# Eight rows of five gradient stores issued from ScalarE in place of GpSimd

## The chip, the core and the metric

The kernel runs on one core of a Trainium2 chip. Its five engines work beside each other, each through its own instructions in order: TensorE (PE) multiplies matrices, VectorE (DVE) and ScalarE (ACT) do element-wise work, GpSimd (POOL) and SyncE (SP) here do little but issue DMAs. A DMA is issued by an engine, is carried by sixteen DMA engines that all issuers share, and reports on a semaphore when it has landed. SBUF is the on-chip memory with 128 partitions (rows), PSUM holds what TensorE produces. The metric is the device time of one execution in microseconds (us), as the median over runs.

## The reference

Attention of one query per head over 8192 keys, and its gradients. There are B x H = 2 x 32 = 64 heads; K and V of a head are 8192 x 128 bf16, which is 2 MB each.

```
scores = einsum("bhqd,bhkd->bhqk", q, k) * d**-0.5
p      = softmax(scores)
out    = einsum("bhqk,bhkd->bhqd", p, v)
dq, dk, dv = vjp(out)(grad_out)
```

With one query row, dv of a head is the outer product of p with grad_out, and dk is the outer product of dS with q, where dS is p times (dP minus its weighted mean) times the scale. So K and V are each read once (268 MB in all), and dK and dV, of the same size, are written once.

## The kernel before

**Tiling.** A head's K is one tile `kvt` of 128 partitions x 64 rows x 128 (16 KB on each partition), and V likewise. Twelve such tiles (`NTILE`) live in SBUF, so six heads are resident. Work is cut into slots. Each head has eight of them (`SL`): in slot r, TensorE transposes one quarter of K (r = 0 to 3) or of V (r = 4 to 7) with eight transposes (L239), ScalarE copies the result from PSUM to SBUF (`ev`, L241), and one slot later TensorE multiplies that copy with the query or with grad_out (`score_chunk`, L260). There are two PSUM buffers for the transposes and two SBUF buffers for the copies. In between run softmax pieces, the sums that give out and dq (`acc`, L420; `pick`, `join`), and the outer products (`outer`, L475 on VectorE), which overwrite a quarter of the V tile or of the K tile in place with dv or dk.

**The pipeline.** The loop at L506 goes through all slots, and in each slot deals with up to four heads at different stages. Head i's dv quarters are formed in its slots 9 to 12 (`O1`), its dk quarters in its slots 13 to 16 (`O0`), counted from its first slot. Each tile is stored when its last quarter is done, and the slot of SBUF that it leaves is loaded again with a tile of head i + 6 (`AHEAD`). A K tile and a V tile take turns in one buffer (`slot_of`): V of head i + 6 goes where K of head i was. A load therefore waits until the store of the tile there has landed.

**Who issues what.** `pin` keeps each engine's instructions in the order of the program. SP issues all loads (L114, one 2 MB DMA each), and for the last head the stores in quarters and the two small results dq and out (L585). GpSimd issues the stores of all other heads (L493). So SP's queue of loads waits on stores, and GpSimd's queue of stores waits on VectorE. ScalarE issues no DMA; per slot it makes one copy of 1.0 us and now and then a small one (`window`, L215) or the exponential (L322).

**The five special dk stores.** For heads 6, 17, 28, 39 and 50 (`SPREAD`) the dk store is cut by partitions. `by_rows` issues rows 8 to 127 with `max_dma_last_dim` set (1920 KB), then rows 0 to 2, 3 to 5 and 6 to 7 as three DMAs of 48, 48 and 32 KB without it (L104). [...] 

**The semaphores of DMAs.** As the records in the trace name them, the DMAs that SP issues carry eight semaphores in turn, and those of GpSimd eight others in turn. A DMA waits for the one that carried its semaphore before, eight DMAs earlier.

Of the kernel before, what the change touches and what calls it, by code (L numbers as in the profile page):

```python
# [21 lines left out]
FIRST = 5  # L22
SPREAD = {
    i: ((8, 128, True), (0, 3, False), (3, 6, False), (6, 8, False)) for i in range(6, 56, 11)
}
BACK = {i + 1: FIRST for i in SPREAD}

@with_exitstack
def kernel(  # L30
# [11 lines left out]
    nc = tc.nc  # L42
    B, H, Sq, D = q.shape
# [5 lines left out]
    NT = Sk // P  # L49
# [6 lines left out]
    store_eng = nc.gpsimd  # L56
    pin = tc.keep_in_program_order
# [30 lines left out]
    def turn(n):  # L88

        if n:  # L90
            parts = turns.pop()
            pin(store_eng.dma_start(out=parts[:n, :], in_=q_rows[:n, : 2 * QT], max_dma_last_dim=2 * QT))
        else:
            pin(store_eng.inc_swdge_sem([], [], mode="reset_dge_cursor"))

    def by_rows(dst, src, steps):

        for step in steps:
            if len(step) == 1:
                turn(*step)  # L100
                continue
            p0, p1, cut = step
            cap = {"max_dma_last_dim": NT * D} if cut else {}
            pin(store_eng.dma_start(out=dst[p0:p1], in_=src[p0:p1], **cap))  # L104

    def load(i, w, pieces=(NCH,)):
        h = heads[i]
        t = kvp.tile([P, NT, D], BF16, tag=f"kv{slot_of(i, w)}", name="kvt")
        h.tile[w] = t
        src = (v_v if w else k_v)[i]  # L110
        c = 0
        for m in pieces:
            n0, n1 = c * CH, (c + m) * CH
            pin(load_eng.dma_start(out=t[:, n0:n1, :], in_=src[:, n0:n1, :]))  # L114
            c += m
# [1 line left out]
    load(0, 0, (1, 1, 2))  # L117

    q_rows = q.rearrange("b h s d -> (b h s) d")
    NTURN = len(BACK) + sum(len(step) == 1 and step[0] > 0 for x in SPREAD.values() for step in x)  # L120
    parts_all = const.tile([CH, NTURN, 2 * QT], BF16, name="parts_all")
    turns = [parts_all[:, n, :] for n in range(NTURN)]

    qd_nat = evp.tile([P, CH, P], BF16, tag="ev", name="qd_nat")
    for w, a in enumerate((q, grad_out)):
        rows = a.rearrange("b h s d -> (b h s) d")
        r0 = FIRST if w == 0 else 0
        if r0:
# [3 lines left out]
                    out=qd_nat[:r0, w, :], in_=rows[:r0], max_dma_last_dim=D  # L132
# [28 lines left out]
    for g in range(SG):  # L161
        nc.vector.tensor_copy(
            out=sel4[g * SW : (g + 1) * SW, :, g // 2, :],
            in_=ident_f[g * SW : (g + 1) * SW, g * SW : g * SW + 2 * NCH].rearrange(
                "p (c t) -> p c t", t=2
            ),
# [9 lines left out]
    for w in range(2):  # L176
        nc.vector.tensor_copy(
            out=qd_pair[:BH, w],
            in_=qd_nat[:BH, w, :]
# [22 lines left out]
    def begin(i):  # L202

        h = heads[i]
        sw = ps_sdp.tile([P, 2 * NT + 2 * P + 4], F32, tag="s", name="sw")
        h.score = (sw[:, 0:NT], sw[:, NT : 2 * NT])
        h.s, h.dp = h.score
        h.mT = sw[0:1, 2 * NT : 2 * NT + P]
        h.qbp = sw[:, 2 * NT + P : 2 * NT + 2 * P]
        h.lsum = sw[:, 2 * NT + 2 * P : 2 * NT + 2 * P + 2]  # L210
        h.mb = sw[:, 2 * NT + 2 * P + 2 : 2 * NT + 2 * P + 3]

    def window(i, w):

        pin(nc.scalar.copy(out=qwin[:, w, :, Q0 : Q0 + 2], in_=qpair[:, w, i]))  # L215

    def broadcast(i, w):

        h = heads[i]
        pin(  # L220
            nc.tensor.matmul(  # L221
                h.qbp,
                lhsT=qT[:, w, i : i + 1].to_broadcast([P, P]),
                rhs=ident_bf,
                start=True,
                stop=True,
            )
        )
        h.qb[w] = small.tile([P, D], BF16, tag=f"qb{w}", name="qb")
        pin(nc.vector.tensor_copy(out=h.qb[w][:], in_=h.qbp))  # L230

    def transpose_chunk(i, c):
        w, c = divmod(c, NCH)
        src = heads[i].tile[w]
        tp = ps_tp.tile([P, CH // 2, P], F32, tag="tp", name="tp")
        for m in range(CH // 2):
            n0 = c * CH + 2 * m
            two = src[:, n0 : n0 + 2, :].rearrange("p n d -> p (n d)").bitcast(F32)
            pin(nc.tensor.transpose(tp[:, m, :], two, ident_f[:]))  # L239
        ev = evp.tile([P, CH // 2, P], F32, tag="ev", name="ev")  # L240
        pin(nc.scalar.copy(out=ev[:], in_=tp[:]))  # L241
        return ev
# [26 lines left out]
    def keep_raw(i):  # L269

        h = heads[i]
        h.rows = work.tile([P, QT * P], F32, tag="rows", name="rows")
        pin(nc.vector.tensor_copy(out=h.rows[:], in_=h.raw[:]))  # L273
# [195 lines left out]
    def outer(i, w, c, ends):  # L469

        h = heads[i]
        n0 = c * CH
        shape = [P, CH, D // 2, 2]
        pin(
            nc.vector.tensor_tensor(  # L475
                out=h.tile[w][:, n0 : n0 + CH, :].rearrange("p n (e t) -> p n e t", t=2),
                in0=h.qb[w][:]
                .rearrange("p (e t) -> p e t", t=2)
                .unsqueeze(1)
                .to_broadcast(shape),  # L480
                in1=h.pair[w][:, n0 : n0 + CH, :].unsqueeze(2).to_broadcast(shape),
                op=ALU.mult,
            )
        )
        if c + 1 in ends:
            at = ends.index(c + 1)
            b0, b1 = (ends[at - 1] if at else 0) * CH, (c + 1) * CH
            dst = (dv_v if w else dk_v)[i]
            if w == 0 and i in SPREAD:
                by_rows(dst, h.tile[w], SPREAD[i])  # L490
            else:
                eng = load_eng if len(ends) > 1 else store_eng
                pin(eng.dma_start(out=dst[:, b0:b1, :], in_=h.tile[w][:, b0:b1, :]))  # L493
# [12 lines left out]
    for g in range(SL * BH + O0 + NCH + 4 - SL):  # L506
        now = [(g // SL - b, g % SL + b * SL) for b in range(4)]
        now = [(i, r) for i, r in now if 0 <= i < BH]

        def at(r0):  # L510

            return next((i for i, r in now if r == r0), None)

        def within(r0):

            return next(((i, r - r0) for i, r in now if r0 <= r < r0 + NCH), None)

        if (i := at(O1 + NCH)) is not None and i + AHEAD < BH:
            load(i + AHEAD, 0)
        if (i := at(O0 + NCH)) is not None and i + AHEAD < BH:  # L520
            load(i + AHEAD, 1)
        if x := within(O1):
            outer(x[0], 1, x[1], last if x[0] == BH - 1 else whole)
        if (i := at(O1 + NCH)) in BACK:
            turn(0)
            turn(BACK[i])
        if x := within(O0):
            outer(x[0], 0, x[1], last if x[0] == BH - 1 else whole)
        ev = None
        if g < SL * BH:  # L530
            i, r = divmod(g, SL)
            if r == NCH:
                begin(i)
                broadcast(i, 1)
            if r == NCH + 2:
                broadcast(i, 0)
            ev = transpose_chunk(i, r)
        if (i := at(A1 + NCH + 2)) is not None:
            join(i, 1)
        if (i := at(A0 + NCH + 2)) is not None:  # L540
            join(i, 0)
        if x := within(A1):
            acc(x[0], 1, x[1])
        if x := within(A0):
            acc(x[0], 0, x[1])
        if (i := at(NCH + 1)) is not None:
            spread_rows(i, 0)
        if (i := at(SL + 1)) is not None:
            spread_rows(i, 1)
        if (i := at(NCH + 3)) is not None:  # L550
            max_spread(i)
            expo(i)
        if prev is not None:
            score_chunk(*prev)
        prev = (g // SL, g % SL, ev) if ev is not None else None
        if (i := at(NCH + 1)) is not None and i + 1 < BH:
            window(i + 1, 0)
        if (i := at(1)) is not None and i > 0:
            window(i, 1)

        if (i := at(NCH)) is not None:
            keep_raw(i)
        if (i := at(SL)) is not None:
            keep_raw(i)
        if (i := at(NCH + 1)) is not None:
            max_part(i)
        if (i := at(NCH + 2)) is not None:
            max_all(i)
        if (i := at(NCH + 4)) is not None:
            normalise_p(i)  # L570
        if (i := at(SL + 1)) is not None:
            weigh(i)
        if (i := at(SL + 2)) is not None:
            normalise_ds(i)
        if (i := at(A1 + NCH)) is not None:
            pick(i, 1)
        if (i := at(A0 + NCH)) is not None:
            pick(i, 0)
# [37 lines left out]
```

## Time and profile before

| | |
|---|---|
| median of 3 runs | 1267.52 us (1266.84 to 1269.59) |
| the profiled execution | 1267.85 us |
| its span, first to last instruction | 1266.1 us |
| TensorE busy | 1187.7 us, 94% |
| VectorE busy | 1031.3 us, 81% |
| ScalarE busy | 557.2 us, 44% |
| GpSimd busy | 80.6 us, 6% |
| moved by DMA | 538.53 MB, mean 425 GB/s |

The profiled execution's own time is 1.75 us over its span, and 0.33 us over the median. The transfers are almost evenly split: SP's queue carries 272.70 MB, GpSimd's 264.25 MB. Store DMAs of 2 MB land 44.9 us (median) after they are issued, loads 20.1 us after. A busy TensorE is not TensorE at its peak, since its matmuls are pipelined and their ends are modelled. Times in views of the trace are microseconds from the span's start. In a timeline, the columns are the start, the time taken, the engine, the line, and the operation with what it writes and reads; in brackets stands how long its engine sat idle before it, and what ended that. "SPq" is SP's queue of instructions.

### The profile page before, as it was taken

The page shows a single profiled execution, that of the slowest core. Times are in us where ns is not written, and L with a number is a line of the kernel's source. Part 1 is how long each engine was busy: PE and PEld are TensorE (multiplying, and loading weights), DVE is VectorE, ACT ScalarE, POOL GpSimd, SP SyncE. Part 2 cuts the span into 40 slices and gives each one's busy share as a digit, 9 for nine tenths or more (in the row PEclk, how much of TensorE's full clock was granted, in tenths as well). Part 3 has the DMA queues.
Part 4 walks back from the last instruction along what each step waited for, and adds up shares of the span by engine and source line. Part 5 has one row for each costly group of instructions (what it writes and reads, how often), then busy time and mean ns, then how long its engine had stood idle before and what let it go on. Part 6 is the DMA issues. An engine that isn't in the chain of part 4 may idle for free.

```text
span 1266.1 us, 24581 instructions
## 1 busy us (share of the span) xinstructions
PE 1187.7 (94%) x10056; PEld 783.1 (62%) x10056; DVE 1031.3 (81%) x2267; ACT 557.2 (44%) x769; POOL 80.6 (6%) x153
## 2 busy tenths in 40 slices
PE   6999999999999999999999999999999999999981
PEld 4666666666666666666666666666666666666650
DVE  3888888888888888888888888888888888887883
ACT  3444444444444444444444444444444444444430
POOL 0000010000010000001000001000000001000000
PEclk9999999999999999999999999999999999999995
DMA  9999999999999999999999999999999999999998
GB/s 393 422 429 429 429 428 429 429 429 429 430 429 428 429 429 429 429 429 429 423 428 430 430 429 428 428 427 430 429 430 428 429 429 427 429 429 429 429 430 336
DMA packets 39741, 538.53 MB, mean 425 GB/s; under 512 B 5236, under 2 KB 5236, under 8 KB 6516
## 3 DMA queue, kind: packets, MB, share of 16 engines
q1 hardware_dynamic: 20172, 272.70, 50.6%
q0 software_dynamic: 19456, 264.25, 49.1%
q8 instruction: 79, 1.29, 0.4%
q14 instruction: 34, 0.28, 0.1%
HBM read 268.47 MB, written 268.47 MB: 424 GB/s over the span
## 4 chain that ended last, share of the span: by engine, by line
PE 68%; DVE 16%; DMA 7%; another core or an unknown queue 4%; issue 2%; ACT 0%; SPq 0%; POOL 0%; ACTq 0%; DVEq 0%
PE tp L239 29%; PE acc L420 17%; PE raw L260 11%; DVE kvt L475 6%; PE sw L280 4%; DMA out_dram<-kvt 4%; DVE sel L443 4%; DVE rows L273 3%; DMA kvt<-in_v_dram 3%; PE sw L366 3%; PE sw L221 2%; PE sw L304 1%; DVE sel L437 1%; PE acc L457 1%
## 5 line engine op out<-in xcount | busy, mean ns | idle before, releaser
L241 ACT COPY ev<-tp 128x1024 f32<-128x1024 f32 x512 | 518.7, 1013 | 660.3 <-PE tp L239 654.8
L475 DVE TENSOR_TENSOR kvt<-qb,pair 128x2048 bf16<-128x2048 bf16 x512 | 617.2, 1216 | 0.2
L239 PE MATMUL tp<-ident_f,kvt 128*128 128x128 f32 x4096 | 547.6, 277 | 3.1 <-DMA kvt<-in_v_dram 2.6
L239 PEld LDWEIGHTS tp<-ident_f,kvt 128*128 128x128 f32 x4096 | 454.0, 144 | 84.2 <-issue 64.6
L260 PE MATMUL raw<-ev,qwin 128*32 128x512 bf16 x2048 | 209.5, 399 | 0.0
L420 PE MATMUL acc<-kvt,dS_pad 128*64 128x512 bf16 x1024 | 160.7, 395 | 0.8 <-DVE dS_pad L406 0.8
L420 PE MATMUL acc<-kvt,E_pad 128*64 128x512 bf16 x1024 | 159.5, 391 | 0.6 <-DVE E_pad L331 0.6
L280 PEld LDWEIGHTS sw<-sel,rows 128*128 128x128 f32 x1024 | 123.9, 191 | 52.4 <-DVE sel L443 25.9
L443 DVE SCALAR_TENSOR_TENSOR sel<-acc,diag,sel 128x128 f32<-128x128 f32 x384 | 134.7, 351 | 13.6
L260 PEld LDWEIGHTS <-qwin 128*32 128x32 bf16 x2048 | 52.7, 93 | 135.4 <-issue 131.0
L280 PE MATMUL sw<-sel,rows 128*128 128x16 f32 x1024 | 136.3, 265 | 0.0
L493 POOL DMA_DIRECT2D out_dram<-kvt x121 | 64.6, 533 | 1062.3 <-DVE kvt L475 484.4
L273 DVE COPY rows<-raw 128x512 f32<-128x512 f32 x128 | 88.6, 692 | 47.0 <-PE raw L260 47.0
L299 DVE TENSOR_REDUCE st<-sw 1x1 f32<-1x128 f32 x64 | 17.8, 278 | 55.9 <-PE sw L298 55.9
L221 PE MATMUL sw<-ident_f,qT 128*128 128x128 bf16 x128 | 28.9, 226 | 36.2 <-DVE st L294 36.2
L420 PEld LDWEIGHTS <-dS_pad 128*64 128x64 bf16 x1024 | 36.6, 108 | 34.9 <-issue 31.8
L366 PEld LDWEIGHTS sw<-st,ones 128*128 128x128 f32 x256 | 37.9, 186 | 31.0 <-issue 15.3
L420 PEld LDWEIGHTS <-E_pad 128*64 128x64 bf16 x1024 | 36.0, 108 | 33.6 <-issue 31.5
L366 PE MATMUL sw<-st,ones 128*128 128x1 f32 x256 | 48.8, 260 | 0.5 <-DVE st L337 0.5
L437 DVE TENSOR_SCALAR sel<-acc,diag 128x128 f32<-128x128 f32 x128 | 43.8, 342 | 0.0
L457 PEld LDWEIGHTS acc<-ones,sel 128*128 128x128 f32 x256 | 39.0, 193 | 7.2 <-DVE sel L443 7.2
L457 PE MATMUL acc<-ones,sel 128*128 128x1 f32 x256 | 36.7, 212 | 6.1 <-DVE sel L443 6.1
(54 smaller groups left out, 381.3 us busy)
## 6 DMA issues: line engine op xcount, KB each, us to landing
out_dram<-kvt POOLq DMA_DIRECT2D x121, 2048.0 KB, 44.9
kvt<-in_v_dram SPq DMA_DIRECT2D x64, 2048.0 KB, 20.1
kvt<-in_k_dram SPq DMA_DIRECT2D x63, 2048.0 KB, 20.2
out_dram<-kvt POOLq DMA_DIRECT2D x5, 1920.0 KB, 49.5
out_dram<-kvt SPq DMA_DIRECT2D x8, 512.0 KB, 20.1
kvt<-in_k_dram SPq DMA_DIRECT2D x2, 512.0 KB, 4.4
kvt<-in_k_dram SPq DMA_DIRECT2D x1, 1024.0 KB, 6.9
out_dram<-kvt POOLq DMA_DIRECT2D x10, 48.0 KB, 49.1
```

Source lines behind the costliest of these rows:

```text
L239: pin(nc.tensor.transpose(tp[:, m, :], two, ident_f[:]))
L241: pin(nc.scalar.copy(out=ev[:], in_=tp[:]))
L260: nc.tensor.matmul(h.raw[g * SW : (g + 1) * SW, :], lhsT=qwin[:, w, e, q0 : q0 + SW], rhs=cols[:, b, :, e], start=(c == 0), stop=(c == NCH ...
L273: pin(nc.vector.tensor_copy(out=h.rows[:], in_=h.raw[:]))
L280: nc.tensor.matmul(h.score[w].rearrange("p (n m t) -> p n m t", m=QT, t=2)[:, :, m, :], lhsT=h.rows[:, m * P : (m + 1) * P], rhs=sel4[:].r ...
L366: nc.tensor.matmul(out, lhsT=ones[:].to_broadcast([P, P]), rhs=col, start=True, stop=True)
L420: nc.tensor.matmul(h.acc[w][g : g + CW, :], lhsT=wts[:, n0 : n0 + CW], rhs=rows[:, n0 : n0 + QT, :].rearrange("p n d -> p (n d)"), start=( ...
L437: nc.vector.tensor_scalar(out=h.sel[:], in0=block, scalar1=diag[:, 0:1], scalar2=None, op0=ALU.mult)
L443: nc.vector.scalar_tensor_tensor(out=h.sel[:], in0=block, scalar=diag[:, b : b + 1], in1=h.sel[:], op0=ALU.mult, op1=ALU.add,)
L457: nc.tensor.matmul(h.acc[w][:, 0:1], lhsT=h.sel[:], rhs=ones[:], start=True, stop=True)
L475: nc.vector.tensor_tensor(out=h.tile[w][:, n0 : n0 + CH, :].rearrange("p n (e t) -> p n e t", t=2), in0=h.qb[w][:] .rearrange("p (e t) -> ...
L493: pin(eng.dma_start(out=dst[:, b0:b1, :], in_=h.tile[w][:, b0:b1, :]))
```

## The change

The three small DMAs of each special store are no longer issued by GpSimd where the store is made. `by_rows` puts them on a list, `pending`. At the head of the next slot, before that slot's loads, outer products, transposes and copies, ScalarE issues what is on the list. [...]

```
-BACK = {i + 1: FIRST for i in SPREAD}
+BACK = {i + 1: (0, FIRST) for i in SPREAD}
...
+    pending = []
+
     def by_rows(dst, src, steps):
...
             p0, p1, cut = step
-            cap = {"max_dma_last_dim": NT * D} if cut else {}
-            pin(store_eng.dma_start(out=dst[p0:p1], in_=src[p0:p1], **cap))
+            if cut:
+                pin(store_eng.dma_start(out=dst[p0:p1], in_=src[p0:p1], max_dma_last_dim=NT * D))
+            else:
+                pending.append((dst[p0:p1], src[p0:p1]))
...
+        for dst, src in pending:
+            pin(nc.scalar.dma_start(out=dst, in_=src))
+        pending.clear()
         if (i := at(O1 + NCH)) is not None and i + AHEAD < BH:
             load(i + AHEAD, 0)
         if (i := at(O0 + NCH)) is not None and i + AHEAD < BH:
             load(i + AHEAD, 1)
...
         if (i := at(O1 + NCH)) in BACK:
-            turn(0)
-            turn(BACK[i])
+            for n in BACK[i]:
+                turn(n)
```

`NTURN`, the count of scrap buffers, is computed for the new form of `BACK` and stays at five.

More of the change, by code (lines that the diff above doesn't have):

```diff
@@ L119 @@
     q_rows = q.rearrange("b h s d -> (b h s) d")
-    NTURN = len(BACK) + sum(len(step) == 1 and step[0] > 0 for x in SPREAD.values() for step in x)
+    NTURN = sum(n > 0 for x in BACK.values() for n in x) + sum(
+        len(step) == 1 and step[0] > 0 for x in SPREAD.values() for step in x
+    )
     parts_all = const.tile([CH, NTURN, 2 * QT], BF16, name="parts_all")
```

## The prediction

> **What bounds the kernel now.** First the page, for the engines, the transfers and what TensorE waits for.
>
> ```profile
> PE 1187.7 (94%) x10056; PEld 783.1 (62%) x10056; DVE 1031.3 (81%) x2267; ACT 557.2 (44%) x769; POOL 80.6 (6%) x153
> ...
> DMA  9999999999999999999999999999999999999998
> ...
> L239 PE MATMUL tp<-ident_f,kvt 128*128 128x128 f32 x4096 | 547.6, 277 | 3.1 <-DMA kvt<-in_v_dram 2.6
> ```
>
> The transfers are full from the first slice to the last, and TensorE's transposes wait for loads only 2.6 us in all. So transfers set the time, and compute keeps just ahead of them. I went further into the packet records of the trace. A 16 KB packet takes 611 ns, and the next of its engine starts 4 ns before it ends; by that they can be strung on sixteen engines. From 20 us on the strings have next to no gaps. They end between 1251.7 and 1264.5 us, the last two at 1263.2 and 1264.5. The small rows lie on the same three strings each time: 15, 15 and 10 rows of 40. One string with 15 is the last to end. The other, which ends at 1259.4, is also the one that carried SP's DMA of 59 query rows, all of them. The two small results land last, at 1265.0, and the span ends 1.07 us later.
>
> Next, who holds the queues. GpSimd's waits, then its timeline around the fifth special store:
>
> ```profile
> POOL out_dram L493 <- DMA out_dram<-kvt: 36.1, 4, 12.3
> POOL out_dram L104 <- DMA out_dram<-kvt: 13.0, 3, 9.2
> ```
>
> ```profile
> 997.61 1.29 POOL L104 DMA_DIRECT2D out_dram<-kvt  x2 [9.47 <-DVE kvt L475]
> 999.37 0.51 POOL L104 DMA_DIRECT2D out_dram<-kvt  x1 [0.47 <-DMA out_dram<-kvt]
> 1009.10 0.51 POOL L104 DMA_DIRECT2D out_dram<-kvt  x1 [9.22 <-DMA out_dram<-kvt]
> 1019.09 0.55 POOL L493 DMA_DIRECT2D out_dram<-kvt  x1 [9.49 <-DVE sel L443]
> ```
>
> The reader is to see that GpSimd stood 9.22 us before the last small DMA, not for data but for a DMA: the one eight before it in its queue, which had the same semaphore. It costs nothing there, since stores land 44.9 us (median) after issue and the transfers have a backlog. SP's loads at that time:
>
> ```profile
> 979.79 0.33 SPq L114 DMA_DIRECT2D kvt<-in_v_dram  x1
> 989.44 0.33 SPq L114 DMA_DIRECT2D kvt<-in_k_dram  x1
> 999.23 0.33 SPq L114 DMA_DIRECT2D kvt<-in_v_dram  x1
> ...
> 1048.31 0.33 SPq L114 DMA_DIRECT2D kvt<-in_k_dram  x1
> 1064.89 0.33 SPq L114 DMA_DIRECT2D kvt<-in_v_dram  x1
> ```
>
> By the loop's order these are V of head 52, K and V of head 53, and K and V of head 56. SP runs far behind the code: the loop asks for K of 56 before the special store of head 50 (997.6 us), and SP issues it at 1048.3.
>
> **Part 1: three DMAs leave GpSimd.** That takes 15 issues of 0.51 us and the 13.0 us of waits at L104 off GpSimd, and part of the 36.1 at L493 and 25.8 at L92 behind them. Worth on the end: nothing, since GpSimd is 6% busy and the backlog covers a store's issue being 9 us earlier. Without that backlog the gain would be at most these waits.
>
> **Part 2: the same bytes in another queue.** Eight rows of 0.611 us on three engines are moved as before, if ScalarE's DMAs are dealt out as SP's are. The trace shows none of three rows from SP; the nearest is the one of 59, all on one engine, which also carried small rows before. Bounds: with the rows gone from the engine that ends last, 1.3 us less (the next ends at 1263.2); with all forty on the one that ends at 1259.4, 25 x 0.61 = 15.2 more there, so 1274.6, or 10.1 us more. I take 0: three rows cannot be split less evenly than one each without a reason. [...]
>
> The rows also land sooner, not behind GpSimd's backlog. The load into that buffer then waits for the 120 rows alone. At the fifth store those landed at 1062.2 us and the last small row at 1064.7, so SP's load at 1064.89 comes 2.5 us earlier. That is worth nothing while no engine has a gap; the load after it waits for its own store anyway.
>
> **Part 3: what ScalarE gets.** The DMAs come after its copy of the slot and ahead of the next:
>
> ```profile
> 996.77 1.01 ACT L241 COPY ev<-tp 128x1024 f32<-128x1024 f32 x1 [0.82 <-PE tp L239]
> 998.91 1.01 ACT L241 COPY ev<-tp 128x1024 f32<-128x1024 f32 x1 [1.12 <-PE tp L239]
> ```
>
> VectorE's last dk quarter is done by 997.3, so for data ScalarE would not wait, and three issues of 0.33 us (SP's rows) fit into the 1.12 us of idle time. If that were all, this part would be 0 too.
>
> But I expect a wait. If ScalarE's DMAs take their turn on SP's eight semaphores, the three wait for the loads eight, seven and six back in the program: with K of 56 the latest, V of 52, K of 53 and V of 53. (Behind them, SP's loads meet a semaphore of ScalarE's at the earliest five loads on, some 48 us later, when rows of 48 KB have long landed: no wait there.) ScalarE runs at compute's pace, SP is late. V of 53 was issued at 999.23 and landed so much later:
>
> ```profile
> DMA to landing us min/median/max: 22.5/22.5/22.5
> ```
>
> So at 1021.7. ScalarE resumes 0.18 us after (as SP's load at 1064.89 after the landing at 1064.71), issues in 0.33, copies in 1.01: 1023.2. Behind it stands the next copy, and TensorE needs that for its matmuls of line 260:
>
> ```profile
> 1000.29 0.41 PE L260 MATMUL raw<-ev,qwin 128*32 128x512 bf16 x4
> ...
> 1002.32 0.41 PE L260 MATMUL raw<-ev,qwin 128*32 128x512 bf16 x4
> ```
>
> The second of these uses it, at 1002.3, which is 4.71 us after the special store. So compute is held for 20.9 us. The same sum for the other four, with V of head i + 3 landed at 164.7, 371.5, 585.0 and 805.4 and the small rows issued at 161.1, 370.2, 579.4 and 788.5: landing plus 1.52 against issue plus 4.71 gives 166.2 against 165.8 (0.4 us), 373.0 against 374.9 (none), 586.5 against 584.1 (2.4), 806.9 against 793.2 (13.7). A landing is a fixed time, as the transfers do not slow, so these delays don't add: after the fifth compute is 20.9 us late in all.
>
> TensorE then stands for some 7 us. At the end of the run, once its work thins out at 1228, the granted clock (third number from the end) falls to half within ten us:
>
> ```profile
> 1230.00:1240.00 10.00, 5.97 (x36) 2.81 (x35) 9.60 (x24) 0.00 (x0) 0.53 (x1) 0.73 1.01 428
> 1240.00:1250.00 10.00, 3.36 (x14) 1.55 (x14) 6.25 (x12) 0.00 (x0) 0.00 (x0) 0.50 1.01 426
> ```
>
> The price of a restart: at the run's start the first 16 transposes took 3.49 us, later 8 take 1.09, so 1.3 us. I take half of it, 0.65, as the trace does not tell whether 7 us are enough. [...]
>
> What is made up: VectorE's and TensorE's pattern repeats every 19.01 us per head. From the transposes at 995.59, 95 slots of 2.376 us bring the last ones to 1221.3; they were at 1226.0, so 4.7 us at the end were spent on late loads. Those are saved, because a late compute finds them landed. Shift at the end: 20.9 + 0.65 - 4.7 = 16.8 us.
>
> ```profile
> 1233.76 11.61 SPq L493 DMA_DIRECT2D out_dram<-kvt  x8
> 1247.34 3.54 SPq L585 DMA_DIRECT2D out_dram<-nat  x2
> ```
>
> The small results are issued from 1264.1, the second by 1264.6. Before, they sat in the backlog and landed at 1265.0. The backlog keeps the slowest engine busy to about 1264.5 still: before, it held 46 us of work at 1218 when loads ended, of which compute had 20 still to hand over; now 25, and the last eighth comes at 1262. A landing without backlog: the fastest row is a first 512 KB load in 4.0 us, of which eight packets of 159 ns are 1.3, so 2.7 for a small one, between 0.4 (no wait past the backlog) and 7.0 (the first grad_out rows). That gives 1267.3, and with 1.07 a span of 1268.4, or 2.3 us more than 1266.1. On the median of 1267.52: **1269.8 us**; own range 1267.4 to 1274.8.
>
> **Rivals.** *No wait, or a hidden one* (not slower). If ScalarE's DMAs have semaphores of their own, or get theirs before K of 56 does, the last one waits for K of 53 at 1011.7 or for nothing. Then compute is 10.9 us late at most, 6.2 after the 4.7, and the results issued by 1254 still sit in the backlog: 1267.5. For it: the transfers hide all but the last 17 us. Against: GpSimd's L104 waits, and that loads of head i + 6 are asked for in the order given. It decides from a shift of some 14 us down.
>
> *The earlier landing helps.* If the load 2.5 us earlier at each store, and the waits off GpSimd, shorten the end, at most the last engine's 1.3 us and some of the lag between strings go: 1264. Against it: no gaps in any string.
>
> *The rows pile up* on one engine: 10.1 us more, 1277.6. For it only the 59 rows.
>
> **How the numbers follow.** About 0.2% (2.5 us) is what a measurement of this kernel can tell from no change. The held compute gets 0.75, and lies across that bound: 0.42 over it, 0.33 within. No wait 0.10, within; earlier landing 0.08, faster; piled rows 0.07, slower. Together faster 0.08, same 0.43, slower 0.49. Range 1266.2 to 1274.6: it leaves out the piled rows, most of the gain and the upper end of the landing.
>
> **What would show it.** ScalarE idle ahead of a copy (L241) for some 17 us after the fourth special store and 10 after the fifth; fewer waits of TensorE for loads at the end; the results (L585) issued near 1264; landings of L585 in a few us. Wrong if ScalarE's largest idle stays near 2.6 us, if loads land later than before because the backlog ran dry during a hold, or if the strings' ends move.

## The result: 1273.59 us, and the profile after

The changed kernel takes 1273.59 us (median of 6 runs, 1270.32 to 1275.95), the kernel before, run beside it, 1267.65 us (6 runs). The ratio is 1.0044, with a 95% interval of 1.0027 to 1.0062: slower by about 5.6 us, which is over the 0.2% that a measurement can tell. The profiled execution took 1270.32 us with a span of 1268.5 us; it is the quickest of the six.

The page of the kernel after: the engines, ScalarE's new queue (packets, MB, share), and the score matmuls, with the idle time ahead of them and what ended it.

```profile
PE 1191.8 (94%) x10056; PEld 785.7 (62%) x10056; DVE 1031.5 (81%) x2267; ACT 557.0 (44%) x769; POOL 73.0 (6%) x138
...
q10 hardware_dynamic: 80, 0.66, 0.1%
...
L266 PE MATMUL raw<-ev,qwin 128*32 128x512 bf16 x2048 | 210.2, 401 | 17.3 <-ACT ev L247 17.3
```

The score matmuls on the page of the kernel before:

```profile
L260 PE MATMUL raw<-ev,qwin 128*32 128x512 bf16 x2048 | 209.5, 399 | 0.0
```

The busy times hardly changed. GpSimd lost 15 instructions, three issues at each of the five stores, and 7.6 us; its five DMAs into `parts_all` are in both traces. New after the change are 40 rows and 40 completions in a third queue, and 17.3 us in which TensorE's score matmuls waited for ScalarE's copy, where before they waited for nothing. What ScalarE waited for stands in its list of waits (line, cause, us in total, times, longest), kernel after:

```profile
ACT ev L247 <- DMA kvt<-in_v_dram: 25.5, 3, 12.4
ACT ev L247 <- PE acc L463: 9.6, 3, 4.1
ACT ev L247 <- DMA out_dram<-kvt: 5.4, 1, 5.4
```

ScalarE's copy has no use for V of a later head. It stood because a DMA issue ahead of it in ScalarE's program waited for a load of V to land. The records of the DMAs name the semaphore: the third issue after the fifth store, which starts at 1020.37 us, waits for number 112. SP's load of 1002.80 us, V of head 53, carried that number and had landed in full at 1020.35. (The 5.4 us that the list puts down to a store are the same wait after the third special store: V of head 31 had landed in full at 585.52, and the third issue began at 585.54.) The timeline of ScalarE after the fourth and the fifth special store:

```profile
791.07 12.78 ACTq L525 DMA_DIRECT2D out_dram<-kvt  x3
803.94 1.01 ACT L247 COPY ev<-tp 128x1024 f32<-128x1024 f32 x1 [12.44 <-DMA kvt<-in_v_dram]
...
1010.70 9.92 ACTq L525 DMA_DIRECT2D out_dram<-kvt  x3
1020.71 1.01 ACT L247 COPY ev<-tp 128x1024 f32<-128x1024 f32 x1 [9.58 <-DMA kvt<-in_v_dram]
```

Three issues, which together took 0.88 us in a later run where nothing held them, took 12.78 and 9.92 us, and the copy follows at once. TensorE resumed behind these copies (timeline of TensorE):

```profile
805.01 0.62 PE L266 MATMUL raw<-ev,qwin 128*32 128x512 bf16 x4 [8.90 <-ACT ev L247]
...
1021.77 0.62 PE L266 MATMUL raw<-ev,qwin 128*32 128x512 bf16 x4 [6.03 <-ACT ev L247]
```

After the fifth store that is 19.5 us later than in the kernel before (1002.32). The end of the run, in SP's queue, kernel after:

```profile
1251.01 10.96 SPq L499 DMA_DIRECT2D out_dram<-kvt  x8
1264.59 1.14 SPq L594 DMA_DIRECT2D out_dram<-nat  x2
```

The small results went out at 1264.59 us in place of 1247.34, so 17.25 us later, and the last one landed at 1266.97 us, against 1265.03 before. Last, the time by stretches (start and end, length, busy time of PE, PEld, DVE, ACT and POOL with counts, then the granted clock, the DMA share and GB/s), kernel after:

```profile
1240.00:1250.00 10.00, 8.12 (x68) 5.07 (x68) 8.09 (x19) 2.42 (x4) 0.53 (x1) 0.94 0.82 349
1250.00:1260.00 10.00, 7.44 (x31) 2.81 (x30) 9.82 (x19) 0.00 (x0) 0.00 (x0) 0.50 0.96 393
```

TensorE and VectorE are still at work here, where before they had all but finished (PE 3.36 us of the first ten, none of the second), and the DMA share is 0.82 where it was 1.01. The transfers wait for compute now. That is the mechanism that the prediction rests on, and in this one execution the sum fits as well. But the median of the runs lies 3.3 us above this execution, and the experiments were made to find that rest.

### The profile page after: what moved, and what is told of

Same layout as the page of the kernel before. It is cut to its first block, busy times and chain, and to the rows that moved or that the text cites. A ratio compares the mean times of both kernels' runs of the same rounds, so it can differ in the third digit from the quotient of the medians.

```text
span 1268.5 us, 24580 instructions
## 1 busy us (share of the span) xinstructions
PE 1191.8 (94%) x10056; PEld 785.7 (62%) x10056; DVE 1031.5 (81%) x2267; ACT 557.0 (44%) x769; POOL 73.0 (6%) x138
## 4 chain that ended last, share of the span: by engine, by line
issue 48%; PE 31%; DMA 9%; DVE 8%; POOL 3%; ACT 0%; POOLq 0%; SPq 0%; ACTq 0%; DVEq 0%
PE tp L245 13%; PE acc L426 7%; DMA out_dram<-kvt 7%; PE raw L266 5%; DVE kvt L481 3%; POOL out_dram L499 2%; PE sw L286 2%; DVE sel L449 2%; DMA kvt<-in_v_dram 1%; DVE rows L279 1%; PE sw L372 1%; PE sw L227 1%; PE sw L310 1%; DVE sel L443 1%; DMA qd_nat<-in_q_dram 1%
## 5 line engine op out<-in xcount | busy, mean ns | idle before, releaser
L266 PE MATMUL raw<-ev,qwin 128*32 128x512 bf16 x2048 | 210.2, 401 | 17.3 <-ACT ev L247 17.3
L266 PEld LDWEIGHTS <-qwin 128*32 128x32 bf16 x2048 | 53.1, 93 | 153.5 <-issue 149.0
L392 DVE TENSOR_SCALAR st<-sw,st 128x1 f32<-128x1 f32 x64 | 14.0, 218 | 41.5 <-PE sw L372 41.5
```

The source lines that it names most:

```text
L266: nc.tensor.matmul(h.raw[g * SW : (g + 1) * SW, :], lhsT=qwin[:, w, e, q0 : q0 + SW], rhs=cols[:, b, :, e], start=(c == 0), stop=(c == NCH ...
```

## The experiments

Each time below is a median; the ratio is to runs of the kernel before on the same chip. The theory is the prediction's: ScalarE's issues wait for SP's loads, and that holds compute. The rival is that the transfers themselves run otherwise once the small rows leave GpSimd's queue.

**The same kernel again**, to see an execution nearer to the median.

> The changed kernel once more, for a second trace and more times. Theory (ScalarE stands before its third small DMA until V of head i + 3 has landed, and compute's tail then sets the end): as before, some 6 us over the kernel before, 1273.6 us; ScalarE idle about 12 us after the fourth special store and 10 after the fifth; the small results issued some 17 us later than in the kernel before, at 1264 us or later. In an execution that is longer than 1270.3 us, the results are issued later by just as much, because the fifth hold ends later or TensorE stands once more. Rival (the transfers themselves got slower by a third queue): the strings of packets end later with the results issued at 1264, or loads land later all along.

1272.97 us, ratio 1.0039 (1.0025 to 1.0054); the profiled execution took 1272.86. SP's queue at its end:

```profile
1267.13 1.14 SPq L594 DMA_DIRECT2D out_dram<-nat  x2
```

The results went out 2.54 us later than in the first execution, and the span is 2.6 us longer: the end hangs on when compute is done. Compute was later since ScalarE stood after more of the stores (7.5, 3.2, 8.3 and 10.4 us), TensorE's clock fell to half three times in place of two (the mean granted clock was 0.983, against 0.986 in the first execution), and loads came 1.2 us later around 990 us. So what differs from run to run is at least in part the loads, and the holds follow them.

**Two of the three, and one of the three, by ScalarE.** The rest stay with GpSimd, so the last wait of ScalarE is for a load one or two places earlier. The diff is that of two; for one, the number is 1.

```
-            else:
+            elif len(pending) < 2:
                 pending.append((dst[p0:p1], src[p0:p1]))
+            else:
+                pin(store_eng.dma_start(out=dst[p0:p1], in_=src[p0:p1]))
```

> Two of the three small DMAs by ScalarE, the rows 6 and 7 by GpSimd as before the change. Theory: the second DMA waits for K of head i + 3, which lands 10 us ahead of V; the hold after the fifth store is about 11 us in all (landing at 1011.7 plus 1.52 against 1002.3), of which 4.7 are made up and the rest is hidden by the backlog: 1267.6 us, no change against the kernel before. Rival (the queue or the issue on ScalarE costs, per DMA): two thirds of the loss, 1271.6 us.

> One of the three small DMAs by ScalarE, the other two by GpSimd. Theory: it waits for V of head i + 2, landed at 1001.7 us, which holds compute by 1 us at most: 1267.6 us, no change. Rival (per DMA): a third of the loss, 1269.6 us.

Two: 1269.6, ratio 1.0010 (1.0001 to 1.0019). One: 1269.49, ratio 1.0010 (1.0002 to 1.0019). After the fifth store ScalarE's copy came at 1012.53 us with two and at 1003.83 with one, in place of 1020.71 with three; it waited for a load of K and one of V, each a place earlier. The results went out at 1256.49 and 1249.64 us, when the backlog of transfers still covers them. By the theory both should then have cost nothing. Both cost some 1.3 us, and the last landings are at 1268.7 and 1266.7 us: a first sign of something beside the hold.

**All three by ScalarE, 14 slots later**, when the loads that they wait for have long landed.

```
+LATE = 14
...
-                pending.append((dst[p0:p1], src[p0:p1]))
+                pending.append((dst[p0:p1], src[p0:p1], now_at[0] + LATE))
...
-        for dst, src in pending:
+        now_at[0] = g
+        while pending and pending[0][2] <= g:
+            dst, src, _ = pending.pop(0)
             pin(nc.scalar.dma_start(out=dst, in_=src))
-        pending.clear()
```

> All three by ScalarE, but 14 slots (33 us) later, when the loads that they wait for have landed (1031 us against 1021.7 after the fifth store). Nothing else of the change is undone: the same rows in the same queue, GpSimd without them, the same semaphores. Theory: no hold, 1267.6 us as in the kernel before; ScalarE's idle times near 2.7 us; the rest of the change is worth nothing either way. Rival (queue, or issue on ScalarE): 1273.6 us as the changed kernel. Rival (GpSimd's waits or the load's earlier start are worth something): below 1265 us.

1274.04, ratio 1.0047 (1.0031 to 1.0064). No issue of ScalarE is held. In SP's queue (kernel with the late DMAs):

```profile
203.19 0.33 SPq L120 DMA_DIRECT2D kvt<-in_v_dram  x1
...
1252.12 3.40 SPq L597 DMA_DIRECT2D out_dram<-nat  x2
```

The results went out at 1252.12, early enough, and yet the last landing is at 1269.8 us, 4.8 later than before. So the hold is not needed for a loss of this size. But the run is not clean: the first line is the load into the buffer of the first special store, at 203.19 in place of 187.63 us, as it had to wait for the late rows. The hold had then to be tried without the rows, and the rows without the hold.

**The hold alone.** GpSimd keeps the small rows; ScalarE issues no DMA, but copies one element of V of head i + 3 at the place where it had its three issues.

```
+        if (i := at(O0 + NCH)) in SPREAD:
+            pin(nc.scalar.copy(out=seen[:, 0:1], in_=heads[i + 3].tile[1][0:1, 0, 0:1]))
```

> The kernel before with its small DMAs on GpSimd, plus one copy of a single element on ScalarE at the place where the change issues its DMAs; the element is of V of head i + 3, so the copy waits for that load and for nothing else. Theory (the wait is all of the loss): ScalarE is held as in the changed kernel, to about 1021 us after the fifth store, and the time is the changed kernel's, some 6 us over the kernel before, 1273.6 us. Rival (the DMAs on ScalarE's queue cost): 1267.6 us, no change, since there are none.

1270.2, ratio 1.0019 (1.0011 to 1.0028). ScalarE's waits, then SP's queue at the end:

```profile
ACT seen L520 <- DMA kvt<-in_v_dram: 26.6, 4, 8.8
```

```profile
1265.86 1.38 SPq L588 DMA_DIRECT2D out_dram<-nat  x2
```

Much the same hold (26.6 us in all, against 25.5, or 30.9 with the 5.4 that stood under a store), results 1.3 us later still than in the kernel after, and 2.4 us more than the kernel before (1.4 to 3.5 by the interval). The prediction's sum for this was 2.3.

**A fourth DMA of 16 bytes by ScalarE** behind the three, so that the last one waits for the load after.

```
+        if pending:
+            pin(nc.scalar.dma_start(out=extra[:, extras.pop(), :], in_=q_rows[:1, : 2 * QT]))
         pending.clear()
```

> The changed kernel with a fourth DMA on ScalarE behind the three, of 16 bytes into a scrap tile. Theory: it waits for K of head i + 4, which lands 10 us after V of i + 3, so the hold after the fifth store ends near 1031 in place of 1021 us and the whole of it shows at the end: 10 us more than the changed kernel, 1283 us. Rival (per DMA or per byte): 2 us more at most, 1275.6 us.

1283.51, ratio 1.0138 (1.0113 to 1.0163).

```profile
ACT ev L249 <- DMA kvt<-in_k_dram: 37.3, 3, 16.4
```

```profile
1276.81 1.13 SPq L598 DMA_DIRECT2D out_dram<-nat  x2
```

One more place in the row of loads is some 10 us more on the path, for 16 bytes. With that and the kernels with one and two DMAs (ScalarE's copy at 1003.83 and 1012.53 us, where it was 1020.71 with three), it is shown what sets the hold here: not the bytes, but which load had the semaphore before.

**The small rows left out.** From here the question is the rest. This kernel does not write rows 0 to 7 of the five special dk outputs. Theory A blames the third queue, theory B the waits that GpSimd no longer makes.

```
-        for dst, src in pending:
-            pin(nc.scalar.dma_start(out=dst, in_=src))
         pending.clear()
```

> The three small DMAs are left out altogether: rows 0 to 7 of the five special dk outputs are not written. Everything else is as in the kernel after, ScalarE issues no DMA. No hold of ScalarE in any theory. Theory A (what slowed the transfers in the run with the late ScalarE DMAs is that a third queue carries rows): that is gone, and 40 packets of 0.611 us with it, so the last string ends at 1262 to 1264.5 as the second string of before did, and the time is 1265 to 1267.6. Theory B (it is that GpSimd lacks the small DMAs, with which it stood 9 us before later stores): still there, 1271 to 1274, last landing 1268 to 1270, and loads of heads 58 and on issued 2 us later than before.

1272.02, ratio 1.0035 (1.0022 to 1.0049): slower by 4.3 us, with no hold, no third queue, and 0.66 MB less to move. GpSimd after the fifth special store, SP's end, and two stretches of the end, all of the kernel without the small rows:

```profile
998.06 0.76 POOL L106 DMA_DIRECT2D out_dram<-kvt  x1 [9.47 <-DVE kvt L481]
1007.07 0.55 POOL L499 DMA_DIRECT2D out_dram<-kvt  x1 [8.25 <-DVE qb L236]
```

```profile
1246.23 3.20 SPq L592 DMA_DIRECT2D out_dram<-nat  x2
```

```profile
1250.00:1260.00 10.00, 0.00 (x0) 0.00 (x0) 0.00 (x0) 0.00 (x0) 0.00 (x0) 0.50 0.67 279
1260.00:1270.00 10.00, 0.00 (x0) 0.00 (x0) 0.00 (x0) 0.00 (x0) 0.00 (x0) 0.50 0.18 72
```

GpSimd issues the next store at 1007 us, where it came to it at 1019 before. Compute is done 1.1 us sooner than before. And while fewer engines are at work from 1250 on (share 0.67, before 0.80), the last packet of data ends at 1266.8 us, 2.3 later than before, in an execution whose span is 2.8 us longer and which is the quickest of its five. So it is one or two engines that are late, not all. Theory A is out: the loss is there without a third queue.

**A third queue that carries nearly nothing.** The kernel before, with ScalarE issuing DMAs of 3, 3 and 2 rows of 16 bytes 14 slots after each special store.

```
+            if not cut:
+                pending.append((p1 - p0, now_at[0] + LATE))
...
+        while pending and pending[0][1] <= g:
+            n = pending.pop(0)[0]
+            into = scrap_all[:n, len(pending) % 3, :]
+            pin(nc.scalar.dma_start(out=into, in_=q_rows[:n, : 2 * QT]))
```

> The kernel before, with GpSimd's small rows as they were, and three DMAs of 3, 3 and 2 rows of 16 bytes from the queries into a scrap tile issued by ScalarE 14 slots after each special store: a third queue that carries nearly nothing. No hold in any theory, as the loads eight back landed long before. Theory A, if the bytes of the third queue matter: as before, 1267.6. Theory A, if a third queue or its semaphores in SP's turn matter by themselves: 1271 to 1274. Theory B: as before, 1267.6.

1268.73, ratio 1.0004 (0.9996 to 1.0013). Results out at 1247.58, last packet 1265.2: as before. A third queue and its semaphores cost nothing that can be seen.

**The small rows by SP**, at the same place, ahead of the loads: `nc.scalar` becomes `load_eng`, nothing else.

> The kernel after with its small rows issued by SP at the same place of the program, ahead of the loads, in place of ScalarE: no third queue, no hold of ScalarE, GpSimd as after. SP reaches them near 1048 us for the fifth store, so they go some 50 us later than before and the load into that buffer waits for their landing, to about 1068 to 1070 in place of 1064.9, which the 20 us of loads that are under way cover. Theory A (third queue): 1267.6, strings end as before, by 1265. Theory B (GpSimd without the small DMAs): 1271 to 1274, last landing 1268 to 1270.

1275.78, ratio 1.0063 (1.0050 to 1.0076). This told nothing on A and B, since SP was hit by itself:

```profile
1034.39 6.04 SPq L525 DMA_DIRECT2D out_dram<-kvt  x3
1089.74 0.36 SPq L118 DMA_DIRECT2D kvt<-in_v_dram  x1
```

The load behind the rows waited for their landing until 1089.74, not 1070 as I had reckoned, so 25 us later than before; all loads queue behind it, the results went out at 1270.52, and nothing covers that.

**GpSimd's waits put back.** The kernel with the late DMAs, and in GpSimd's queue, where the rows stood, DMAs of as many rows of 16 bytes.

```
                 pending.append((dst[p0:p1], src[p0:p1], now_at[0] + LATE))
+                into = scrap_all[: p1 - p0, p0 // 3, :]
+                pin(store_eng.dma_start(out=into, in_=q_rows[: p1 - p0, : 2 * QT], max_dma_last_dim=2 * QT))
```

> The kernel with ScalarE's three DMAs 14 slots late (no hold), and in GpSimd's queue, where its small rows stood, three DMAs of 3, 3 and 2 rows of 16 bytes into a scrap tile. So GpSimd makes the same waits as before, and the rows still go by ScalarE's queue. Theory B (GpSimd lacks the waits of its small DMAs, issues the next stores some 12 us sooner, and the stores then take the share of the loads): mended, 1267.6 to 1268.7, stores of the fifth at 1019 and 1041 as before, last landing 1265 to 1266, and loads not behind those of before at 220 us. Theory A (rows on a third queue): still 1272 to 1274.

1272.06, ratio 1.0031 (1.0019 to 1.0043). GpSimd made its waits again (the store after the fifth special one at 1025.27 us), and the loss stayed. The load at 203 us stayed late too, however, so B is weakened by this and not out.

**More waits.** The kernel before, each small DMA of GpSimd followed by one of 16-byte rows (the two lines that the last diff adds, behind the row DMA).

> The kernel before with each small row DMA of GpSimd followed by one of as many rows of 16 bytes into a scrap tile, so that six semaphores of eight in place of three are taken and the next stores come later still. Theory B, if later stores are worth something by the same way: loads 1 MB ahead of before at 220 us, time 1266 to 1267.5. If the waits of before are already enough: 1267.6 to 1268.7. If GpSimd is held so long that stores run out: above 1269. Theory A: 1267.6.

1274.84, ratio 1.0057 (1.0043 to 1.0072). Later stores are no gain: what 16 KB packets took above 0.611 us each sums to 165 us over all engines from 20 us on, in place of 87 before, and by 1060 us the loads are 1.4 MB behind.

**The waits without the rows.** The kernel before, with the row DMAs replaced in place by DMAs of 16-byte rows. Rows 0 to 7 of the five special dk outputs are not written here either. Against the kernel before it has DMAs of a few bytes in place of the rows; against the one without small rows it adds these DMAs and GpSimd's waits for them.

```
-            pin(store_eng.dma_start(out=dst[p0:p1], in_=src[p0:p1], **cap))
+            if cut:
+                pin(store_eng.dma_start(out=dst[p0:p1], in_=src[p0:p1], **cap))
+            else:
+                into = scrap_all[: p1 - p0, p0 // 3, :]
+                pin(store_eng.dma_start(out=into, in_=q_rows[: p1 - p0, : 2 * QT], max_dma_last_dim=2 * QT))
```

> The kernel before with the three small row DMAs of GpSimd replaced, in place, by three of 3, 3 and 2 rows of 16 bytes into a scrap tile: GpSimd makes its waits as before, but the rows are not in its queue, and rows 0 to 7 of the five special dk outputs are not written. ScalarE issues nothing, no hold. Theory B, that the waits of the small DMAs keep the transfers together: about as before, 1266 to 1268, and the eight strings that carry TensorE's instructions end within 2 us of each other. Theory C, that it is the rows' bytes in GpSimd's queue, which put three other strings behind at each special store so that the slow packets fall there: as without them altogether, 1271 to 1273, one of those eight strings ending 4 us or more after the others with 9 us of slow packets in place of 4 to 5.

1272.34, ratio 1.0031 (1.0018 to 1.0044). GpSimd after the fifth special store, and the end:

```profile
999.09 0.59 POOL L108 DMA_DIRECT2D scrap_all<-in_q_dram  x1
1004.11 0.56 POOL L108 DMA_DIRECT2D scrap_all<-in_q_dram  x1 [4.43 <-DMA out_dram<-kvt]
1013.82 0.56 POOL L108 DMA_DIRECT2D scrap_all<-in_q_dram  x1 [9.14 <-DMA out_dram<-kvt]
1026.61 0.59 POOL L498 DMA_DIRECT2D out_dram<-kvt  x1 [12.23 <-DVE qb L235]
```

```profile
1250.00:1260.00 10.00, 0.00 (x0) 0.00 (x0) 0.00 (x0) 0.00 (x0) 0.00 (x0) 0.50 0.80 332
1260.00:1270.00 10.00, 0.00 (x0) 0.00 (x0) 0.00 (x0) 0.00 (x0) 0.00 (x0) 0.50 0.27 108
```

GpSimd waits again, 9.14 us ahead of the third small DMA, where it was 9.22. Its next store goes out 14.9 us after the fourth special one (15.7 in the kernel before, 9.0 without the small rows) and 28.3 us after the fifth (21.5 and 9.0). The waits are not those of before to the microsecond, but near them up to the fourth store, and the loss is that of the kernel without the rows. Of the slow packets on its last string (below), those outside the regular ones fall mostly ahead of the fifth store, at 608 and 824 to 833 us. So B is out. What matters is that the rows themselves, 40 packets of 16 KB, lie in GpSimd's queue.

**Where it shows.** Strung on sixteen engines as in the prediction, the packets of these runs give the table below. Eight strings also carry packets of instructions (queue q8 on the page), nine or ten of some 0.95 us each; in the kernel without the small rows they end at 1261.4 us or later, the other eight between 1249.7 and 1262.6. "Ends" are those of the packets of data and their completions. "Slow" is what the 16 KB packets of the string that is last of these eight took above 0.611 us each, summed; some 4 us of that are the regular ones, ten packets that stand beside one of instructions.

| kernel | ends of the other seven, us | last of the eight, us | its slow packets, us |
|---|---|---|---|
| before | 1261.6 to 1263.0 | 1263.2 | 4.4 (all eight 3.9 to 4.8) |
| small rows left out | 1261.4 to 1263.2 | 1266.8 | 9.4 |
| waits without the rows | 1263.2 to 1266.8 | 1268.3 | 10.0 |
| late DMAs | 1263.3 to 1267.4 | 1269.2 | 10.8 |
| late DMAs and GpSimd's waits | 1261.3 to 1264.7 | 1268.2 | 10.3 |

In the kernel before, all eight end within 1.6 us. In each of the four without the rows in GpSimd's queue, one of them took 5.0 to 6.4 us more in slow packets and ends 1.5 to 3.5 us behind the next, and it is the last of all sixteen. It ends 2.3 to 4.7 us after the last packet of the kernel before (1264.5, on a string with small rows), and the spans of these four executions are 2.8 to 5.2 us longer. In the two other kernels that keep the rows in GpSimd's queue, the hold alone and the nearly empty third queue, no string of the eight has more than 5.9 us of slow packets; with one and with two DMAs moved, the highest have 9.2 and 10.7. Each figure is of one execution. The bursts of slow packets come between 595 and 1080 us, some 30 to 80 us after the third, fourth and fifth special stores: without the rows four packets at 609 to 616, 3.4 us in all over 0.611 each, with the late DMAs six packets of 0.9 to 2.4 us in a row at 1056 to 1065. The kernel before has such bursts too, but nearly all on strings that end 5 us or more before the last.

## Why the prediction was right, and where it was short

The range held the time, and the likeliest case, a held compute, was the one that came. But the median lies in the upper part of the range, which reached to 1274.6 us because the small results might take almost 7 us to land. They took 1.8 us behind the last issue, and what filled the range was a loss that the prediction had put at nothing. In this respect it is luck that the range held. By its steps:

- **What bounds the kernel**: right. The transfers set the end of every kernel in which neither compute nor the loads were held, and in the kernel after they run dry (share 0.82 at 1240 to 1250) because compute is late.
- **Part 1, GpSimd's issues and waits, 0**: right. GpSimd's busy time fell by 7.6 us and its waits for DMAs are gone from its list; with the waits in place and the rows gone the time was the same as without either (1272.34 and 1272.02).
- **Part 2, the same bytes in another queue, 0, between -1.3 and +10.1**: this is the step that failed. On the engines it held: the rows lie on the same three strings as before, 15, 15 and 10. That three rows would lie on three engines was my estimate alone, as the trace before had no DMA of three rows by SP; I took it for the whole matter. No run shows the 0 for the end. That the rows leave GpSimd's queue costs 4.3 us by the run without them and 4.4 by the run with the waits in their place (2.3 to 6.2 us by the two intervals). A nearly empty third queue cost nothing that can be seen (ratio 1.0004), but the bytes taken out of GpSimd's queue changed how evenly the engines ended: the last of the eight strings was 1.5 to 3.5 us behind the next, where before all eight ended within 1.6. "The load 2.5 us earlier" came as said: 185.1 in place of 187.6 us at the first store, and no gain from it.
- **Part 3, the wait**: right in kind, and near in size. ScalarE waited for V of head i + 3: 12.44 and 9.58 us of idle after the fourth and fifth stores (I had some 17 and 10 for these). TensorE was 19.5 us late after the fifth store (20.9), the results went out 17.25 us late (16.8 for the shift, 1264.1 and 1264.6 for the issues, against 1264.59 for the first), and the span of the profiled execution is 1268.5 (1268.4). A hold by itself cost 2.4 us (2.3). That the span agrees to 0.1 us is luck in part, as terms of the sum were off both ways: second issue, landing and the rest behind it were 1265.2 + 1.8 + 1.6 in place of 1264.6 + 2.7 + 1.07, and the shift at the end is the next point.
- **The clock restart, 0.65 taken**: too low. In the fourth and fifth holds TensorE idled 8.90 and 6.03 us, and both times the granted clock fell to half (0.5), for 10.2 us from 798.3 and 6.8 us from 1020.1. So either idle time was enough, and the whole 1.3 us of the run's start, of which I had taken half, was nearer, but low as well: set against the same matmuls of the kernel before, those of L266 were 11.8 us late when TensorE went on after the fourth store and 13.4 soon after, and 19.45 and 21.7 at the fifth, so the time at half clock cost 1.6 and 2.3 us. From 1100 us on the 21.7 shrank to 17.2, so 4.5 us were made up (4.7). The shift 20.9 + 0.65 - 4.7 = 16.8 was thus, as measured, 19.45 + 2.3 - 4.5 = 17.25: a hold that came out 1.4 us shorter hid the dearer restart.
- **The rivals**: no wait, or a hidden one, is what the kernels with one and two DMAs were built to be, and there the results did sit in the backlog. The rows did not pile up on one engine. That the earlier landing helps was not seen.

What the forecast of 1269.8 lacked is a second term of about 4 us, in Part 2. Whether the two add up in full can't be told: 2.4 and 4.3 are 6.7, and the kernel after lost 5.6 by its ratio, with 3.4 to 7.9 as its interval. A reason why they might not is that in its trace only 9.4 of the sixteen engines are busy, on average, from 1246 to 1248 us, as compute is late; a slow engine could catch up there. In its two profiled executions the one of those eight strings with most slow packets (7.1 and 9.0 us) was not the last to end. How much of the 5.6 us is due to each is therefore argued and not shown. That the runs of this kernel spread over 5.6 us, where six of the kernel before spread over 2.8, would fit a loss that hangs on which engine a burst falls on; this is not shown either.

## What stays open

Why the slow packets fall on a string that ends early when the rows are in GpSimd's queue, and on one that ends last when they are not. The obvious story, that the rows put their three strings behind so that the bursts fall there, isn't borne out: in the kernel before those three have 0.8 to 2.8 us of slow packets in the whole run. Nor was it tried to give the strings with the packets of instructions fewer rows, which would show what such a string is worth.

## What to carry to other kernels

Before a DMA is given to an engine that computes, find out which earlier DMA its semaphore belonged to: here the issue waited for that one, in order, with all the engine's work behind it (three issues took 9.92 us after the fifth store, 0.88 where nothing held them), and one place in the row was worth 10 us. A cost of 0 for "the same bytes on the same engines" needs a look at what each queue holds next to them; where the transfers set the end, it was that of the slowest of sixteen engines (in the kernel before, the last packet at 1264.5 us in a span of 1266.1), and 5 to 6 us of slow packets on one of them went with a span 3 to 5 us longer. And profile a second execution when the profiled one is at the edge of the runs: the first here agreed with the sum to 0.1 us, and the median did not.

## What was not expected of the hardware

A kernel that moves 0.66 MB less, with all its instructions else unchanged, was slower by 4.3 us (ratio 1.0035, 1.0022 to 1.0049).

A 16 KB packet, which takes 0.611 us nearly always, can take 0.9 to 2.4 us, in bursts on one engine. They are much more frequent where an engine has served GpSimd's queue alone for a while: among GpSimd's packets that follow six or more of its own in a row on their string, while loads still run, 3% took over 0.8 us in the kernel before, 5% without the small rows and 15% with the late DMAs (12 of 362, 8 of 147 and 16 of 111, so few in number), while among those that alternate with SP's it is under 0.4%, nearly all of them beside a packet of instructions. It is not the only condition, as the burst at 609 to 616 us without the rows fell among alternating packets.
